# Linear attention with a token and a channel mixer: all operations in another explicit order, batch 1's sums of values ahead of the first channel mix, two thirds of the clamps on GpSimd

## The chip, the core and the metric

The kernel runs on one core of one Trainium2 chip. The metric is the device time of one execution in microseconds (us). The core has TensorE (PE, matrix products, with its weight loads as PEld), VectorE (DVE), ScalarE (ACT), GpSimd (POOL), and the queue engine SyncE (SP), which issues nearly all transfers. Each engine runs its own instructions in the order in which they stand; engines wait for one another by semaphores.

## What is computed

The reference takes `q`, `k`, `v` of 4 batches, 4 heads, 1088 positions and 32 dimensions, two sketches `S1`, `S2` (8 x 32), and four mixer weights that come in as float32. Cut to what matters:

```python
phi(x) = einsum('i,j->ij', S1 x, S2 x)            # 64 features per position
kv  = einsum('bhsf,bhsd->bhfd', phi(k), v);  z = phi(k).sum(s)
x   = (phi(q) @ kv) / (phi(q) @ z + 1e-6)         # (4, 1088, 128)
h   = relu(x.T @ w_tok1) @ w_tok2                 # token mixer: 1088 -> 256 -> 1088
u   = x + h.T
out = u + relu(u @ w_ch1) @ w_ch2                 # channel mixer: 128 -> 1536 -> 128
```

## The kernel before, in words

**Inputs.** The four weights arrive as 64-bit doubles and are turned to float32 by integer steps in `convert` (names `w<weight><piece>`: weight 0 and 1 are the token mixer's, 2 and 3 the channel mixer's). The steps of a piece are `.abs` (L270 on DVE or POOL, L272 on ACT), `.low` (L276, ACT), `.sign` (L281 on ACT, L284 on DVE), `.clamp` (L287, DVE or POOL), `.merge` (L290, DVE) and `.add` (L294 or L296, POOL). A piece is then split in a high and a low half, `.hi` (L377, ACT) and `.lo` (L380, DVE or POOL), so that a float32 product is made as three fast matmuls. There are 20 pieces, so 20 clamps beside that of the sketch `s`.

**Stages of a batch b.** `Kb.p0` and `Kb.p4` (L407, PE) project the keys, `Kb.c0` and `Kb.c4` (ACT L418) copy, `Kb.v0`, `Kb.v4`, `Kb.v8` (DVE L428) make the 64 features. **`Kb.s` (L448, PE) sums keys times values**: for b > 0 that is one run of 72 small matmuls; the profile records each float32 matmul in two passes, so it counts 144. `Kb.kvz` (ACT L457) takes the result. `Qb` makes the query features (batch 0 by `Q0.p`, `Q0.a` and `Q0.m`; later batches by `Qb.p`, L497, and by transfers `Qb.w` and `Qb.r`, L606 to L622). `Ab.x` (L652, PE, 72 recorded matmuls of 66 columns) gives numerators and denominators, `Ab.d` (DVE L663 to L666) divides, `Ab.t` (L702 for batch 0, L708 else) and `Ab.w` (L824, L828) are the token mixer, `Ab.hT` its transpose, `A0.u` (L733) adds the residual, `A0.uh` and `A0.ul` (ACT L799, DVE L802) split u.

**The channel mix** `Ui` works on spans of 384 (the last two: 288) columns of u; three spans are batch 0's. For each of its 12 pieces of the hidden size, `Ui.f` (L878) is three matmuls into a bank `ps_h`, `Ui.h` (ACT L882) takes the relu, `Ui.l` (DVE L885) the low half, and `Ui.s` (L891) three matmuls into `ps_o`. A group of three such matmuls is called a **triple** below; there are 288 triples in the kernel, 12 x 12 x 2. `ps_h` has three banks, and the `.sign` step on ACT takes one as well, so that `Ui.f` and the conversion of the weights pass the banks on to each other.

**The order.** `ORDER` (L63 and on) is a list of all operations by name; `Plan.run` emits them in it, and so it decides the order on each engine, on the transfer queues, and, where a name carries `:dve`, `:pool` or `:act`, the engine. `fill:n` puts n matmuls without use on PE, which keep it from standing idle; eight more stand at the very start. No instruction is computed by another rule: the lines that set it are

```python
        for entry in ORDER:
            name, _, e = entry.partition(":")
...
            op = named[name].pop(0)
...
            op.emit(e or next(iter(op.ways)))
```

Of the kernel before, what the change touches and what calls it, by code (L numbers as in the profile page):

```python
# [63 lines left out]
d00 s d10 q0 s.low s.abs w00.low w00.abs:dve s.sign:dve s.clamp s.merge s.add w00.clamp:pool Q0.s0:pool w00.sign:dve w00.merge w00.add w10.abs:act  # L64
w10.low Q0.s1:act d01 w10.clamp:dve w10.sign:act w10.merge w01.abs:dve w10.add w01.low fill:4 Q0.p00 Q0.p01 Q0.a00 Q0.a01 w01.sign:act Q0.m00 Q0.m01
w01.clamp:dve w01.merge Q0.p20 Q0.a20 k0 d02 K0.p0 K0.p4 Q0.p21 K0.c0 s.rows w02.abs:pool w02.clamp:pool K0.c4 w02.low Q0.a21 d04 w02.sign:act v0
K0.v0 Q0.m20 K0.v8 Q0.m21 K0.v4 d03 q1 d05 fill:2 Q0.p10 Q0.p11 K0.s00 K0.s04 K0.s08 K0.s10 K0.s14 K0.s18 w04.abs:act Q0.a10 Q0.a11 w04.low w01.add
w02.merge w02.add w04.clamp:dve Q0.m11 Q0.m10 w03.abs:act w03.low w04.sign:act K0.kvz w03.clamp:dve w05.abs:dve w05.clamp:pool w04.merge w03.sign:act
Q1.p d13 w03.merge Q1.c0 w05.low Q1.c1 w13.abs:act w05.sign:act w13.low w13.sign:act A0.x0 w04.add d11 d12 d30 d20 k1 d21 d22 d14 d31 d32 q2 d23 v1
Q1.w0 Q1.w1 d15 d33 w03.add A0.d0 A0.x1 w13.clamp:dve w05.merge A0.d1 w13.merge w05.add A0.x2 A0.t0 A0.d2 A0.t1 A0.t2 w11.abs:act w11.low w12.low  # L70
w12.abs:act w30.abs:act w11.sign:act w30.low w12.sign:act w30.sign:act A0.relu w13.add K1.p0 A0.hT K1.p4 w11.clamp:dve w20.abs:dve w12.clamp:dve
w30.clamp:dve w11.merge w12.merge w30.merge w20.clamp:pool w11.add w20.low K1.c0 w20.sign:act w12.add w30.add w21.abs:act w21.low K1.c4 A0.hTh
w21.sign:act w22.low w30.hi K1.v0 w20.merge w20.add w20.hi w20.lo:pool w22.abs:act K1.v4 w21.clamp:dve w30.lo:dve K1.v8 w21.merge fill:1 A0.u0 A0.u1
A0.w0 A0.w1 A0.uh00 w22.sign:act w31.abs:act A0.ul00 w22.clamp:dve w14.abs:dve U0.f U0.f Q2.p w21.add w21.hi w21.lo:pool w22.merge w22.add A0.uh11
A0.ul11 U1.f U0.h w31.low U0.l U0.h U0.l w32.low w32.abs:act w31.clamp:dve w31.sign:dve w14.clamp:dve w32.clamp:dve w31.merge U1.h w22.hi w32.sign:act
# [926 lines left out]
```

## Time and profile before

| | |
|---|---|
| time, median of 3 runs | 217.52 us (216.55 to 217.95) |
| time of the profiled execution | 218.62 us |
| span in its profile | 216.8 us |
| PE busy | 209.7 us, 97% of the span |
| DVE, ACT, POOL busy | 144.9, 118.7, 64.5 us |

A slice of the page is 1/40 of the span. PE counts as busy from the start of a matmul to its modelled end, so that a stretch of matmuls that wait a little for one another still reads as busy; what the stretch is worth is read from the start of one group to the start of the next. A row of the timeline merges neighbouring instructions of one line: its start, its length, the engine, and in brackets the idle time ahead of it with what ended it.

### The profile page before, as it was taken

The page shows a single profiled execution, that of the slowest core. Times are in us where ns is not written, and L with a number is a line of the kernel's source. Part 1 is how long each engine was busy: PE and PEld are TensorE (multiplying, and loading weights), DVE is VectorE, ACT ScalarE, POOL GpSimd, SP SyncE. Part 2 cuts the span into 40 slices and gives each one's busy share as a digit, 9 for nine tenths or more (in the row PEclk, how much of TensorE's full clock was granted, in tenths as well). Part 3 has the DMA queues.
Part 4 walks back from the last instruction along what each step waited for, and adds up shares of the span by engine and source line. Part 5 has one row for each costly group of instructions (what it writes and reads, how often), then busy time and mean ns, then how long its engine had stood idle before and what let it go on. Part 6 is the DMA issues. An engine that isn't in the chain of part 4 may idle for free.

```text
span 216.8 us, 5259 instructions
## 1 busy us (share of the span) xinstructions
PE 209.7 (97%) x2069; PEld 195.0 (90%) x2069; DVE 144.9 (67%) x305; ACT 118.7 (55%) x282; POOL 64.5 (30%) x73
## 2 busy tenths in 40 slices
...
GB/s 229 399 407 399 402 357 204 194 179 248 29 216 242 197 165 17 108 186 238 182 101 0 3 3 60 172 61 0 30 5 2 42 36 3 24 0 0 51 0 54
DMA packets 11472, 28.44 MB, mean 131 GB/s; under 512 B 1336, under 2 KB 5432, under 8 KB 11448
## 3 DMA queue, kind: packets, MB, share of 16 engines
q1 hardware_dynamic: 11304, 27.85, 41.1%
q8 instruction: 16, 0.26, 0.5%
q10 hardware_dynamic: 144, 0.26, 0.4%
...
## 4 chain that ended last, share of the span: by engine, by line
PE 87%; DMA 4%; DVE 2%; issue 2%; SPq 2%; ACT 1%; ACTq 0%
PE ps_h L878 34%; PE ps_o L891 33%; DMA doubles<-wt 4%; PE ps_a L708 4%; PE ps_a L828 4%; PE ps_a L652 3%; PE ps_a L448 2%; PE ps_a L824 2%; SPq L252 1%; PE ps_a L702 1%; PE ps_a L407 1%; DVE c L290 1%; PE ps_a L497 1%; DVE k_p L428 1%; PE ps_a L733 1%
## 5 line engine op out<-in xcount | busy, mean ns | idle before, releaser
L885 DVE SCALAR_TENSOR_TENSOR hl<-ps_h,hh 128x384 fp32r<-128x384 f32 (+2 forms) x144 | 74.9, 532 | 59.6 <-ACT hh L882 58.5
L882 ACT ACTIVATE hh<-ps_h 128x384 fp32r<-128x384 f32 (+2 forms) x144 | 67.7, 475 | 75.4 <-PE ps_h L878 54.5
L878 PE MATMUL ps_h<-uh,halves 128*128 128x384 f32 (+2 forms) x288 | 87.6, 335 | 0.0
L891 PE MATMUL ps_o<-hh,halves 128*128 128x384 f32 (+2 forms) x288 | 71.5, 330 | 0.0
L878 PEld LDWEIGHTS ps_h<-uh,halves 128*128 128x128 f32 x288 | 53.8, 190 | 1.0 <-ACT hh L882 0.4
L891 PEld LDWEIGHTS ps_o<-hh,halves 128*128 128x128 f32 x288 | 50.6, 189 | 0.2
L878 PE MATMUL ps_h<-ul,halves 128*128 128x384 f32 (+2 forms) x144 | 47.7, 331 | 0.0
L891 PE MATMUL ps_o<-hl,halves 128*128 128x384 f32 (+2 forms) x144 | 47.3, 328 | 0.0
L878 PEld LDWEIGHTS ps_h<-ul,halves 128*128 128x128 f32 x144 | 27.4, 190 | 0.2 <-DVE ul L802 0.2
L891 PEld LDWEIGHTS ps_o<-hl,halves 128*128 128x128 f32 x144 | 27.2, 189 | 0.0
L802 POOL TENSOR_TENSOR ul<-us,uh 128x320 fp32r<-128x320 f32 (+3 forms) x8 | 6.6, 821 | 57.6 <-ACT uh L799 47.4
L294 POOL TENSOR_TENSOR whole<-c,tail 128x384 int32<-128x384 int32 (+3 forms) x12 | 11.8, 995 | 9.1 <-DVE c L290 7.8
L676 POOL TENSOR_TENSOR xl<-x,xh 128x384 fp32r<-128x384 f32 x7 | 7.1, 1019 | 22.6 <-ACT xh L672 22.6
L632 POOL TENSOR_TENSOR qp<-qp,br 128x544 f32<-128x544 f32 x8 | 10.9, 1369 | 6.2 <-PE ps_o L891 4.5
L428 DVE TENSOR_TENSOR k_p<-ps_a,a_sb 128x1024 f32<-128x1024 f32 (+1 forms) x12 | 11.4, 950 | 0.5 <-ACT a_sb L418 0.4
L276 ACT ACTIVATE tail<-doubles 128x256 int32<-128x256 uint32 (+3 forms) x20 | 10.9, 552 | 0.7 <-DMA doubles<-wt 0.7
L652 PEld LDWEIGHTS ps_a<-kvz,qp 128*64 128x64 f32 x288 | 8.9, 137 | 2.0 <-issue 0.9
L652 PE MATMUL ps_a<-kvz,qp 128*64 128x66 f32 x288 | 9.8, 223 | 0.5 <-issue 0.3
L290 DVE SCALAR_TENSOR_TENSOR c<-c,ps_h 128x512 int32<-128x512 int32 (+3 forms) x17 | 9.3, 559 | 1.1 <-ACT ps_h L281 0.8
L708 PE MATMUL ps_a<-halves,xh 128*128 128x256 f32 x54 | 9.9, 280 | 0.0
L281 ACT ACTIVATE ps_h<-doubles 128x512 int32<-128x512 f32 (+3 forms) x17 | 9.2, 543 | 0.0
L380 POOL TENSOR_TENSOR halves<-whole,halves 128x384 fp32r<-128x384 f32 (+3 forms) x7 | 8.1, 1177 | 2.4 <-ACT halves L377 2.4
...
## 6 DMA issues: line engine op xcount, KB each, us to landing
...
```

The costliest lines, as they stand in the source:

```text
L276: nc.scalar.activation(t["tail"], low.bitcast(U32), AF.Copy, scale=2.0 ** -29)
L281: nc.scalar.activation(t["sign"], f32(high), AF.Prelu, scale=2.0 ** -19, alpha=2.0 ** 70)
L290: nc.vector.scalar_tensor_tensor(t["c"], t["c"], 3, t["sign"], op0=ALU.logical_shift_left, op1=ALU.bitwise_or)
L294: engines[e].tensor_tensor(dst(), t["c"], t["tail"], op=ALU.add)
L428: nc.vector.tensor_tensor(t["k_p"][:pn, t0 * H:t1 * H], a.unsqueeze(3).broadcast_to([pn, n, R, R]), t["sb", base][:pn, at:at + n].unsqueez ...
L632: engines[e].tensor_tensor(qp[:, p, cs], qp[:, p, cs], t["br"][:, p, cs], op=ALU.mult)
L652: nc.tensor.matmul(x_ps[c:c + 64, o:o + 2 * (D + 1)], lhsT=qp[:, p, s0 + c:s0 + c + 64], rhs=kvz_all[b % 2][:, p, :], start=True, stop=True,)
L708: nc.tensor.matmul(t["h_ps"][:, :DTOK], lhsT=t[l][:m, i, :], rhs=part(0, piece, r, j * DTOK, DTOK)[:m], start=(i == 0 and k == 0), stop=(i ...
L878: nc.tensor.matmul(h_ps[:, :cn], lhsT=part(2, at[2][e][0], l, at[2][e][1] * P, P), rhs=r[:, :cn], start=(m == 0), stop=(m == 2))
L882: nc.scalar.activation(t["hh"][:, :cn], t["h"][:, :cn], AF.Relu)
L885: nc.vector.scalar_tensor_tensor(t["hl"][:, :cn], t["h"][:, :cn], 0.0, f32(t["hh"][:, :cn]), op0=ALU.max, op1=ALU.subtract)
L891: nc.tensor.matmul(outs[i][:, :cn], lhsT=part(3, at[3][e][0], l, at[3][e][1] * P, P), rhs=r[:, :cn], start=(e == 0 and m == 0), stop=(e == ...
```

## The change

The table `ORDER` is replaced as a whole; no other line differs. One pair of places of it:

```diff
@@ -61,53 +61,53 @@
 ORDER = """
...
-U1.l w32.merge w31.add w14.low w31.hi w14.sign:act Q2.c0 U0.s U0.s w14.merge K1.s U0.f U0.f U1.s w22.lo:pool w31.lo:pool w32.add U0.h w15.low U0.h
...
+w20.lo:dve w31.abs:dve w31.clamp:pool fill:2 A0.u0 A0.w0 w22.abs:act w30.hi w31.low w21.merge w21.add w22.clamp:pool A0.uh00 A0.ul00 K1.s A0.u1 U0.f
...
```

All 288 triples, all transfers and all steps of the conversion are still there. There is one `fill` more (eight in place of seven beside the first eight). Of the 20 clamps of the weights, POOL has 14 (5 before) and DVE 6 (15 before). DVE has nine `.abs` (seven before) and one `.sign` (three before), and it makes one of the two spreads of the sketch that POOL made.

On TensorE, here is the place of batch 1's sums (L448) in the program before; `whole` and `halves` are converted weights, `hTl` the token mixer's hidden layer:

```order
L497 MATMUL ps_a<-q_sb,s_rows 32x272 x8
L878 MATMUL ps_h<-uh,halves_511 128x384
L878 MATMUL ps_h<-ul,halves_511 128x384
L878 MATMUL ps_h<-uh,halves_511 128x384
L891 MATMUL ps_o<-hh,halves_505 128x384 x2
L891 MATMUL ps_o<-hl,halves_505 128x384
L891 MATMUL ps_o<-hh,halves_505 128x384 x2
L891 MATMUL ps_o<-hl,halves_505 128x384
L448 MATMUL ps_a<-v_sb,k_p 32x33 x72
L878 MATMUL ps_h<-uh,halves_564 128x384
```

and in the change, where it is followed by the rest of the token mixer:

```order
L733 MATMUL ps_a<-ident,x 128x128 x3
L824 MATMUL ps_a<-whole_287,hTl 128x384
L824 MATMUL ps_a<-whole_491,hTl 128x384
L448 MATMUL ps_a<-v_sb,k_p 32x33 x72
L733 MATMUL ps_a<-ident,x 128x128 x3
L878 MATMUL ps_h<-uh,halves_509 128x384
L878 MATMUL ps_h<-ul,halves_509 128x384
L878 MATMUL ps_h<-uh,halves_509 128x384
L824 MATMUL ps_a<-whole_516,hTl 128x384
L824 MATMUL ps_a<-whole_441,hTl 128x384
```

The sums stand behind five triples of the channel mix before, and ahead of the first one in the change; the token mixer's second chunk (`A0.w1`, the last two rows) went behind the first triple. In matmuls as the profile counts them, 336 stand ahead of the sums before and 299 in the change. `A0.w2` (the third chunk) stands behind 17 triples and `A1.x` behind 36 in both.

On GpSimd, this is the conversion of the token mixer's weights in the program before (L287 are clamps, L294 adds):

```order
L294 TENSOR_TENSOR whole_285<-c,tail 128x256
L294 TENSOR_TENSOR whole_288<-c,tail 128x512
L287 TENSOR_SCALAR c<-c 128x256
L294 TENSOR_TENSOR whole_346<-c,tail 128x512
L294 TENSOR_TENSOR whole_369<-c,tail 128x512
L294 TENSOR_TENSOR whole_398<-c,tail 128x256
L294 TENSOR_TENSOR whole_448<-c,tail 128x384
L287 TENSOR_SCALAR c<-c 128x256
L294 TENSOR_TENSOR whole_482<-c,tail 128x384
```

and in the change:

```order
L287 TENSOR_SCALAR c<-c 128x512
L294 TENSOR_TENSOR whole_314<-c,tail 128x512
L287 TENSOR_SCALAR c<-c 128x512
L294 TENSOR_TENSOR whole_333<-c,tail 128x512
L287 TENSOR_SCALAR c<-c 128x256
L294 TENSOR_TENSOR whole_422<-c,tail 128x512
L287 TENSOR_SCALAR c<-c 128x384
L294 TENSOR_TENSOR whole_426<-c,tail 128x256
L294 TENSOR_TENSOR whole_441<-c,tail 128x384
L287 TENSOR_SCALAR c<-c 128x384
L294 TENSOR_TENSOR whole_491<-c,tail 128x384
```

A clamp now stands ahead of nearly every add. On SyncE's queue, the transfers around batch 1's values (`v_sb`; `q_sb` here is batch 2's) stand like this before:

```order
L252 DMA k_sb<-kT 128x1152
L252 DMA doubles_94<-wc 128x256
L252 DMA doubles_98<-wc 128x512
L252 DMA doubles_102<-wt 128x320
L252 DMA doubles_95<-wc 128x256
L252 DMA doubles_99<-wc 128x512
L252 DMA q_sb<-qT 128x1088
L252 DMA doubles_100<-wc 128x512
L252 DMA v_sb<-v 128x1188
```

and in the change:

```order
L252 DMA k_sb<-kT 128x1152
L252 DMA doubles_94<-wc 128x256
L252 DMA doubles_98<-wc 128x512
L252 DMA doubles_95<-wc 128x256
L252 DMA v_sb<-v 128x1188
L252 DMA doubles_102<-wt 128x320
L252 DMA doubles_99<-wc 128x512
```

The values moved ahead of three pieces of weights and of batch 2's queries.

## Rows read from the trace of the kernel before

**Rows 1.** The page, busy time of each engine (its share of the span, and the number of instructions).

```profile
PE 209.7 (97%) x2069; PEld 195.0 (90%) x2069; DVE 144.9 (67%) x305; ACT 118.7 (55%) x282; POOL 64.5 (30%) x73
```

**Rows 2.** Busy time of each engine in three stretches that follow each other; the last three numbers are TensorE's granted clock, the share of the DMA engines' time, and what they moved in GB/s.

```profile
14.00:29.50 15.50, 14.31 (x208) 10.62 (x205) 14.50 (x34) 14.19 (x37) 10.84 (x13) 1.00 1.03 400
29.50:45.10 15.60, 13.96 (x217) 12.59 (x216) 11.29 (x26) 12.76 (x30) 8.08 (x9) 0.89 0.84 219
45.10:213.60 168.50, 168.47 (x1551) 165.12 (x1550) 109.03 (x225) 81.77 (x193) 39.10 (x36) 1.00 0.29 83
```

**Rows 3.** TensorE's timeline, the rows around the start of the channel mix (L878, L891), around batch 1's sums (L448) and at the third chunk of the token mixer (L824, 45.09).

```profile
21.38 2.96 PE L702 MATMUL ps_a<-whole,x 128*128 128x256 f32 x12 [0.21 <-DVE x L666]
24.27 0.69 PE L407 MATMUL ps_a<-s_c,k_sb 128*64 128x64 f32 x16
...
26.58 0.88 PE L733 MATMUL ps_a<-ident,x 128*128 128x128 f32 x6 [0.20 <-DVE k_p L428]
27.30 2.75 PE L824 MATMUL ps_a<-whole,hTl 128*128 128x384 f32 x8
29.58 0.63 PE L878 MATMUL ps_h<-uh,halves 128*128 128x384 f32 x1
...
31.01 0.69 PE L497 MATMUL ps_a<-q_sb,s_rows 64*32 64x272 f32 x16
...
33.40 1.59 PE L448 MATMUL ps_a<-v_sb,k_p 128*32 128x33 f32 x138
36.63 0.26 PE L448 MATMUL ps_a<-v_sb,k_p 128*32 128x33 f32 x6 [1.64 <-issue]
36.82 0.44 PE L878 MATMUL ps_h<-uh,halves 128*128 128x384 f32 x1
...
41.09 0.51 PE L891 MATMUL ps_o<-hh,halves 128*128 128x384 f32 x2
...
42.15 0.49 PE L733 MATMUL ps_a<-ident,x 128*128 128x128 f32 x3
42.40 0.60 PE L891 MATMUL ps_o<-hh,halves 128*128 128x384 f32 x2
...
45.09 1.24 PE L824 MATMUL ps_a<-whole,hTl 128*128 128x320 f32 x4
```

**Rows 4.** The chain of waits, two pieces of the dense part (start, length, what; x6 is two triples).

```profile
50.57 1.04 PE ps_o L891 x6
51.61 0.52 PE ps_h L878 x3
```

**Rows 5.** Busy time in two short stretches, columns as in rows 2: the one with the sums, and the one behind it.

```profile
33.40:36.80 3.40, 1.76 (x145) 1.60 (x144) 2.33 (x6) 2.68 (x7) 2.57 (x3) 1.00 0.79 216
36.80:41.10 4.30, 4.30 (x22) 4.28 (x17) 1.44 (x4) 2.43 (x5) 2.15 (x3) 0.60 1.01 194
```

**Rows 6.** TensorE's timeline, the attention of batch 0 in two pieces (x59 and x13 of 72 matmuls).

```profile
16.58 2.23 PE L652 MATMUL ps_a<-kvz,qp 128*64 128x66 f32 x59 [0.16 <-ACT kvz L457]
19.11 0.57 PE L652 MATMUL ps_a<-kvz,qp 128*64 128x66 f32 x13 [0.30 <-issue]
```

**Rows 7.** The page's row of the queue that carries instructions (packets, MB, share), and the same queue's row in two windows of half a microsecond, 33.5 to 34.0 and 40.5 to 41.0 us; its windows beside these have no row.

```profile
q8 instruction: 16, 0.26, 0.5%
...
q8 instruction: 1, 0.02, 16.2%
...
q8 instruction: 1, 0.02, 20.2%
```

**Rows 8.** DVE's timeline, from the last division of batch 0 to the split of its first chunk of u.

```profile
22.16 0.56 DVE L666 TENSOR_TENSOR x<-ps_a,rec 128x384 f32<-128x384 f32 x1
...
23.22 0.75 DVE L287 TENSOR_SCALAR c<-c 128x384 f32<-128x384 f32 x2
23.89 1.33 DVE L290 SCALAR_TENSOR_TENSOR c<-c,ps_h 128x384 int32<-128x384 int32 x3
25.30 1.23 DVE L428 TENSOR_TENSOR k_p<-ps_a,a_sb 128x1024 f32<-128x1024 f32 x1
...
28.10 0.42 DVE L380 TENSOR_TENSOR halves<-c,halves 128x256 fp32r<-128x256 f32 x1
28.44 0.42 DVE L428 TENSOR_TENSOR k_p<-ps_a,a_sb 128x256 f32<-128x256 f32 x1
28.77 0.41 DVE L290 SCALAR_TENSOR_TENSOR c<-c,ps_h 128x256 int32<-128x256 int32 x1
29.30 0.56 DVE L802 TENSOR_TENSOR ul<-ps_a,uh 128x384 fp32r<-128x384 f32 x1
```

**Rows 9.** A clamp on DVE and what GpSimd did meanwhile, from the two engines' timelines.

```profile
18.69 1.37 DVE L287 TENSOR_SCALAR c<-c 128x384 f32<-128x384 f32 x1
...
17.33 2.52 POOL L294 TENSOR_TENSOR whole<-c,tail 128x512 int32<-128x512 int32 x2 [0.19 <-DVE c L290]
```

**Rows 10.** Groups by line and shape (times seen, then busy us and mean ns of one): clamps on the two engines.

```profile
L287 DVE TENSOR_SCALAR c<-c 128x512 f32<-128x512 f32 x5 | 2.4, 471 | 0.0
L287 POOL TENSOR_SCALAR c<-c 128x256 f32<-128x256 f32 x3 | 1.2, 415 | 4.2 <-DVE c L270 4.2
L287 POOL TENSOR_SCALAR c<-c 128x512 f32<-128x512 f32 x2 | 1.2, 615 | 1.5 <-DVE c L270 1.4
```

**Rows 11.** The page's group of the channel mix's low halves on DVE (columns as in rows 10; what stands behind the bar is idle time ahead of them and its releaser).

```profile
L885 DVE SCALAR_TENSOR_TENSOR hl<-ps_h,hh 128x384 fp32r<-128x384 f32 (+2 forms) x144 | 74.9, 532 | 59.6 <-ACT hh L882 58.5
```

More of the change, by code (lines that the diff above doesn't have):

```diff
@@ L63 @@
 ORDER = """
[L64 to L75, printed above, removed]
@@ L108 @@
-U10.h U10.l U10.h U10.l U11.f U11.f U10.s U11.h U11.l U11.h U11.l U11.h U11.l U11.f U10.s U11.h U11.l U11.f U11.s U10.f U11.s U10.f U11.s U11.s U11.h
-U11.l U10.h U10.l U10.h U10.l U10.f U10.h U10.l U11.f U11.s U10.s U11.f U11.f U10.s U11.h U11.l U10.s U11.f U11.h U11.h U11.h U11.l U11.l U10.ol U11.l
-U11.s U11.f U11.h U11.s U11.s U11.s U11.l U11.s U11.ol U10.out U11.out
+d00 s q0 d01 k0 d10 v0 d02 s.low s.abs s.sign:dve s.clamp s.merge s.add Q0.s0:dve w00.low Q0.s1:act w00.abs:act w00.sign:act w01.abs:dve
@@ new lines @@
+w01.clamp:pool w00.clamp:pool w00.merge fill:4 Q0.p00 Q0.p01 w01.low Q0.a00 Q0.a01 Q0.p20 w01.sign:act Q0.a20 Q0.m00 Q0.m01 w01.merge w10.abs:pool
+w10.clamp:pool w00.add w01.add K0.p0 K0.p4 K0.c0 w10.low K0.c4 s.rows Q0.a21 w10.sign:act Q0.p21 K0.v0 K0.v4 w10.merge d03 K0.v8 Q0.m20 Q0.m21
+w02.abs:act w02.low w02.sign:act d04 fill:1 K0.s00 fill:1 K0.s04 Q0.p10 K0.s08 K0.s10 Q0.p11 K0.s14 K0.s18 Q0.a10 w03.low w04.low w03.abs:dve
+w02.clamp:dve w02.merge w04.abs:dve w10.add q1 d13 d05 w03.clamp:pool Q1.p w03.sign:act Q0.m10 w03.merge Q0.a11 K0.kvz Q0.m11 w04.sign:act w02.add
@@ new lines @@
+w04.clamp:pool w04.merge Q1.c0 Q1.c1 w05.abs:act w05.low w13.abs:act w13.low w05.sign:act w13.sign:act w03.add d11 d20 d30 d12 A0.x0 A0.x1 A0.d0 A0.d1
+A0.x2 A0.t0 A0.t1 w05.clamp:pool w05.merge k1 d21 d22 d31 v1 d14 d32 Q1.w0 Q1.w1 q2 d15 d23 d33 Q1.r0None Q1.r00 Q1.r01 Q1.r1None Q1.r10 Q1.r11
+w04.add w13.clamp:pool w13.merge w05.add A0.d2 w11.abs:act w11.low w11.sign:act w20.low w13.add A0.t2 K1.p0 K1.p4 w20.abs:dve w12.abs:act w30.low
+w12.low w20.sign:act w12.sign:act A0.relu K1.c0 w11.clamp:dve w30.abs:dve w11.merge w20.clamp:dve w30.clamp:dve w12.clamp:pool w20.merge w12.merge
```

68 lines of the change are left out of this document (37 added, 31 removed).

## The prediction

> **What bounds the kernel now.** I read the page first, then the engines' busy time by stretches, then TensorE's timeline. TensorE is busy for 209.7 of 216.8 us [rows 1], which says little by itself, so the stretches matter. From 45.1 us on it is busy for 168.47 of 168.50 us at full clock [rows 2]: there nothing but TensorE's own work counts, and both kernels have the same work. What a new order can win lies ahead of that. From 14.0 to 29.5 us DVE is busy for 14.50, ACT for 14.19 and GpSimd for 10.84 of 15.5 us while the transfers run at 400 GB/s [rows 2]: the weights are converted there, and TensorE waits for what comes out. From 29.5 to 45.1 us TensorE is busy for 13.96 of 15.60 us at a granted clock of 0.89 [rows 2].
>
> TensorE's timeline shows the largest hole. Batch 1's sums start at 33.40, 138 of their 144 matmuls run, then TensorE stands for 1.64 us, with no engine named, and six more run from 36.63 [rows 3]. Behind it the granted clock falls: 0.60 in the mean of 36.8 to 41.1 us, a mixture of the levels 2.4 and 1.2 GHz, against 1.00 until 36.8 [rows 5].
>
> **A point where the two can be compared.** `A0.w2`, the third chunk of the token mixer, stands behind 17 triples of the channel mix in both orders, and ahead of it the same other work is done (but for one fill). Before, it starts at 45.09 [rows 3]. If it starts earlier in the change and nothing new waits behind it, the whole kernel ends earlier by as much.
>
> **What is lost before that point.** From the first triple (29.58) to 45.09 there are 15.51 us [rows 3]. The work in them: 17 triples at 0.52 us [rows 4] are 8.84; the query projection `Q2.p` 0.62 (31.01 to 31.63, its row is 0.69 long with the overlap); the sums 1.6 (1.59 for 138); `A0.u2` 0.25 (42.15 to 42.40) [rows 3]. That makes 11.3, and 4.2 us are lost. Of these 1.64 are the hole. The slow clock costs 1.67: from 36.82 to 41.09, 4.27 us [rows 3], five triples ran, worth 2.60 [rows 4]. Some 0.9 are small waits, half of it at the first triple, whose low half of u is ready only at 29.86 [rows 8].
>
> **Why the hole is there, and whether it stays.** The engine waits for nothing the profile names, in the middle of one run of matmuls that no wait divides. The instruction queue has 16 packets for the kernel, 0.26 MB [rows 7], with 2069 matmuls and as many weight loads [rows 1]: a packet for about 129 matmuls. One starts between 33.5 and 34.0, the next between 40.5 and 41.0 [rows 7]. The hole comes after 336 + 138 = 474 matmuls (336 stand ahead of the sums). A smaller stop of 0.30 us, also without a releaser, comes after 59 of the 72 matmuls of batch 0's attention [rows 6], which 162 matmuls precede: 221. The distance is 253, two packets within the records' errors. So I read the hole as TensorE running out of instructions at a packet's border. Borders are then near 346 and 474: the sums cover 336 to 480, take 128 matmuls in 1.42 us, and reach the second border before the packet has come, which takes 1.42 + 1.64 = 3.06 us.
>
> In the change 299 matmuls stand ahead of the sums. The border at 346 falls inside them, the one at 474 comes 31 matmuls after their end, behind `A0.u1`, `A0.w1`, `A0.u2` and seven triples. From border to border that is 97/144 of 1.6 = 1.1, and 0.44 + 1.14 + 0.25 + 3.64 = 5.5 (half of 0.88 and half of 27.30 to 29.58 for the first two [rows 3]), 6.6 us in place of 1.42. So the hole and the slow clock behind it should be gone: 3.3 us.
>
> The Trainium skill has a rule on this, in "Runtime: NRT & Kernel Launch", section "Instruction fetch mechanics": instructions come in blocks of 256 while the previous block runs, and crossing a block's border is mostly hidden. By that rule the hole would be no matter of the border and would go wherever the sums go; it would leave the sum 3.3 us worse. The distance of 253 matmuls [rows 6] agrees with blocks of that size, the 1.64 us [rows 3] don't agree with "hidden".
>
> **What the change costs ahead of the first triple.** Batch 1's sums now stand in front of it, so they wait for their own inputs with the whole channel mix behind them. Values: they were queued behind 1.9 MB more (three weight pieces and batch 2's queries); at 400 GB/s [rows 2] they land 4.7 us sooner, so no wait is likely for them. Products: `K1.v0`, `v4`, `v8` on DVE. I take the end of `A0.t2` as unchanged (24.3, 21.38 + 2.96 [rows 3]), since the loads, the query features and the divisions that feed it stay in their sequence; bounds 23.6 and 25.0, as DVE does fewer clamps but GpSimd more.
>
> Between the last division (22.16 + 0.56) and `K1.v0` (25.30) DVE has one abs, three clamps and three merges [rows 8]; in the change one abs more, which I take as 0.3 (above zero, and below the 0.42 that a split of as many columns takes [rows 8]). So `K1.v0` ends at about 26.8 (before 26.54). `A0.u0` waits for that bank as it did (26.58 [rows 3]) and takes 0.44, `A0.w0` 1.14, to 28.4; the `fill:2` lies inside that wait (uncovered it costs 0.6). On DVE one merge, `v4` and `v8` follow, 0.41 + 1.2 + 0.4 [rows 8]: 28.8. The sums run from 28.8 to 30.4, `A0.u1` to 30.8. DVE meanwhile makes a low half (0.42), an abs, a merge (0.41) and u's low half (0.56) [rows 8], ready near 30.4. **The first triple starts near 30.8, not 29.58**, but with the sums already done.
>
> From there to `A0.w2`: 17 triples 8.84, `Q2.p` 0.62, `A0.w1` 1.14, `A0.u2` 0.25, together 10.85, so 41.65 without any wait. ACT and DVE are near full there and each pass of a bank of `ps_h` through a sign and a merge can hold a triple: I allow 0.5 (before: 0.9), bounds 0 and 2. `A0.w2` starts at 42.15, **2.9 us earlier**.
>
> **The clamps.** Nine go from DVE to GpSimd. DVE gets up to 0.47 us back for each; on GpSimd a clamp takes 0.42 (256 columns) or 0.62 (512) [rows 10], some 4.7 us for nine. None is in the sum: DVE's relief is what keeps `K1.v0` where it was although GpSimd is in its way. That way is seen at 18.69: a clamp of 384 columns took 1.37 us while GpSimd ran two adds until 19.85 [rows 9], where clamps of 512 columns take 0.47 in the mean [rows 10].
>
> **Behind 45 us.** Both engines' pieces moved there, but TensorE waited 0.03 us in 168.5 [rows 2], so a new order can only add: I allow 0.3.
>
> **Sum.** 2.9 - 0.3 = 2.6 us less than the profiled execution's 218.62, so 216.0 for one like it; that execution stands 1.1 above the median of 217.52. From the median: **214.9 us**.
>
> **Rivals.**
>
> *Clamps on GpSimd hold up DVE (slower).* Ten operations of DVE that GpSimd can hold up as at 18.69 stand between the third piece of weights and `K1.v8`. GpSimd, busy for 10.84 of 15.5 us [rows 2], gets about 3.6 us more there (seven clamps at 0.52) and would be at 93%. If half of them wait 0.9 as that clamp did (1.37 against 0.47 [rows 9, 10]), DVE is 4.5 us later, less some 1.5 of relief (four clamps at 0.47, less one abs): the sums start 3 us later with TensorE idle in front of them, and the clock falls as it did behind the hole, 1.67 more. That turns -2.6 into +2.1: 219.6. It decides from 1.0 us of lateness on, where the clock goes with it. Against it: the mean of DVE's five clamps of 512 columns is 0.47 [rows 10], so none of these waited so long. The Trainium skill states this lock in "SBUF — State Buffer", section "SBUF: two separate sides": whichever of the two starts holds the pair of ports for the whole instruction. The row at 18.69 agrees. Chance 0.13.
>
> *The stop stays (no change).* Either the hole belongs to the sums themselves and goes where they go, or the packet comes too late for the new place as well: behind the hole the next one starts 4 us after the border (36.63 to 40.5 [rows 3, 7]), and if it needs the 2.6 us from 34.0 to 36.63 again, that is 6.6 us, just the time there is. Then an idle stretch of up to 1.6 and the slow clock come back: 3.3 - 2.6, 218.2; with a shorter stop 217. The rule of the Trainium skill quoted above, "Runtime: NRT & Kernel Launch", stands on the side of the first half of this rival. Chance 0.16.
>
> *A new wait in the dense part (no change).* `A2.t0` stands 7 triples behind `A2.x`, before 19. Its cover is 3.6 us. On DVE two divisions (at least 0.56 each, their last step) and a low half (0.42 for 256 columns, here 384) [rows 8] stand in it, some 1.8 at the least; with four low halves of the mix among them (0.53 each [rows 11]) it is 3.9, TensorE idles for 0.3 or more, and where the clock falls too some 2.2 are gone: 217.1. Chance 0.13.
>
> **Chances and range.** The forecast has 0.58; its own range is 213.4 (no wait ahead of `A0.w2`, front 0.7 earlier, nothing lost behind) to 216.2. A measurement of this kernel can tell about 1% (2.2 us) from no change; of the 0.58 some 0.50 lies beyond that. Faster 0.50, slower 0.16 (the first rival and a little of the others), the same 0.34. For 8 in 10 the range goes from 213.2 to 219.0, which leaves out most of the first rival.
>
> **What would show it.** In the profile of the change: the sums start near 29 and run in one piece of 144; the first triple near 30.8; no granted clock below 1.00 from 30 to 45 us; `A0.w2` near 42.2; from there to the end 168.5 us as before. The forecast is wrong if TensorE stands for over 1 us ahead of the sums, if an idle stretch without a releaser comes some 31 matmuls behind them, or if waits appear beyond 45 us.

## The result and the profile after

The changed kernel takes 218.86 us (median of 12 executions, 218.18 to 219.80), the kernel before 217.59 in the same session (12 executions, 216.55 to 222.46). The ratio is 1.0061 with a 95% interval of 1.0040 to 1.0081: 0.6% slower, where 214.9 us had been forecast. The time lies inside the range of 213.2 to 219.0, at its upper end, and on the wrong side of no change. Beside two of the experiments the ratio was 1.0047 (1.0021 to 1.0074) and 1.0021 (0.9983 to 1.0058).

Ratios leave out executions that stand over 1.5% above the fastest of their kernel, and the kernel before has many of those. Of its 90 executions beside the experiments 38 had a granted clock of 0.997 or more and took 217.1 to 220.1 us (median 217.8); the other 52 had a lower one and took 219.0 to 229.0 (median 222.0). Over all 90 the median is 220.5. All 30 executions of the changed kernel, those of the result included, had 0.997 or more and took 217.8 to 220.0 (median 218.9). So the changed kernel is about 1 us slower than an execution of before at full clock, and steadier.

The profiled execution of the changed kernel took 218.18 us, its span is 216.4. The page's busy row and row of the granted clock (tenths, 40 slices), answering to [rows 1]:

```profile
PE 209.7 (97%) x2070; PEld 192.8 (89%) x2070; DVE 147.5 (68%) x301; ACT 117.8 (54%) x282; POOL 63.5 (29%) x77
...
PEclk9999999999999999999999999999999999999999
```

The three stretches of [rows 2], in the changed kernel:

```profile
14.00:29.50 15.50, 14.40 (x329) 10.62 (x325) 14.15 (x33) 12.92 (x35) 12.32 (x16) 1.00 1.04 401
29.50:45.10 15.60, 14.42 (x94) 11.21 (x83) 12.43 (x24) 14.70 (x36) 11.25 (x14) 1.00 0.74 224
45.10:213.00 167.90, 167.90 (x1547) 164.36 (x1545) 112.65 (x227) 80.75 (x190) 33.91 (x32) 1.00 0.31 83
```

The clock is 1.00 throughout, and in the middle stretch TensorE is busy for only 0.46 us more than before, although there is no stop: other waits have come in its place. TensorE's timeline shows them (answering to [rows 3]):

```profile
26.77 1.46 PE L824 MATMUL ps_a<-whole,hTl 128*128 128x384 f32 x4
28.15 1.45 PE L448 MATMUL ps_a<-v_sb,k_p 128*32 128x33 f32 x144
29.54 0.55 PE L733 MATMUL ps_a<-ident,x 128*128 128x128 f32 x3
30.77 0.44 PE L878 MATMUL ps_h<-uh,halves 128*128 128x384 f32 x1 [0.68 <-ACT uh L799]
31.36 0.45 PE L878 MATMUL ps_h<-ul,halves 128*128 128x384 f32 x1 [0.15 <-DVE ul L802]
31.65 0.33 PE L878 MATMUL ps_h<-uh,halves 128*128 128x384 f32 x1
31.82 1.45 PE L824 MATMUL ps_a<-whole,hTl 128*128 128x384 f32 x4
33.10 0.49 PE L733 MATMUL ps_a<-ident,x 128*128 128x128 f32 x3
...
40.56 0.34 PE L891 MATMUL ps_o<-hl,halves 128*128 128x384 f32 x1
41.17 0.44 PE L878 MATMUL ps_h<-uh,halves 128*128 128x384 f32 x1 [0.27 <-DVE c L290]
...
43.92 1.24 PE L824 MATMUL ps_a<-whole,hTl 128*128 128x320 f32 x4
```

The sums run in one piece of 144. Then TensorE waits for `A0.uh00`. ACT's timeline says why it is late: `w22.abs` (L272) stands ahead of it and waits 1.86 us for one of the four `c` buffers, which `w20.lo` on DVE gives up when it ends at 28.98 (28.57 and 0.41 long).

```profile
26.74 0.42 ACT L377 CAST halves<-c 128x256 fp32r<-128x256 f32 x1
29.02 0.70 ACT L272 ACTIVATE c<-doubles 128x512 f32<-128x512 f32 x1 [1.86 <-DVE halves L380]
29.63 0.39 ACT L377 CAST halves<-c 128x256 fp32r<-128x256 f32 x1
29.92 0.43 ACT L276 ACTIVATE tail<-doubles 128x256 int32<-128x256 uint32 x1
30.26 0.46 ACT L799 CAST uh<-ps_a 128x384 fp32r<-128x384 f32 x1
```

The pause ahead of 41.17 is a bank of `ps_h` that `w15.merge` (L290, the second one here) gives up late: on DVE it stands behind a low half (L380) of 1.37 us, while GpSimd runs from 39.27 to 40.16 and from 40.28 to 41.31.

```profile
39.34 1.37 DVE L380 TENSOR_TENSOR halves<-c,halves 128x512 fp32r<-128x512 f32 x1
40.64 0.47 DVE L290 SCALAR_TENSOR_TENSOR c<-c,ps_h 128x320 int32<-128x320 int32 x1
...
39.27 0.89 POOL L294 TENSOR_TENSOR whole<-c,tail 128x320 int32<-128x320 int32 x1 [0.38 <-DVE c L290]
40.28 1.03 POOL L380 TENSOR_TENSOR halves<-whole,halves 128x256 fp32r<-128x256 f32 x1
```

So `A0.w2` starts at 43.92, 1.17 earlier than in the profile of before and not 2.9. At the last matmul 0.42 of this is left (212.86 against 213.28).

### The profile page after: what moved, and what is told of

It is laid out like the page before. It is cut to its first block, busy times and chain, and to the rows that moved or that the text cites. A ratio compares the mean times of both kernels' runs of the same rounds, so it can differ in the third digit from the quotient of the medians.

```text
span 216.4 us, 5250 instructions
## 1 busy us (share of the span) xinstructions
PE 209.7 (97%) x2070; PEld 192.8 (89%) x2070; DVE 147.5 (68%) x301; ACT 117.8 (54%) x282; POOL 63.5 (29%) x77
## 4 chain that ended last, share of the span: by engine, by line
PE 84%; DVE 5%; ACT 5%; issue 3%; POOL 1%; DVEq 0%
PE ps_h L878 33%; PE ps_o L891 33%; PE ps_a L708 4%; PE ps_a L828 4%; PE ps_a L652 3%; PE ps_o L248 2%; DVE k_p L428 2%; ACT tail L276 2%; DVE c L290 2%; PE ps_a L407 1%; PE ps_a L448 1%; POOL whole L294 1%; ACT ps_h L281 1%; ACT c L272 1%; PE ps_a L537 1%
## 5 line engine op out<-in xcount | busy, mean ns | idle before, releaser
L885 DVE SCALAR_TENSOR_TENSOR hl<-ps_h,hh 128x384 fp32r<-128x384 f32 (+2 forms) x144 | 74.1, 531 | 42.7 <-ACT hh L882 42.1
L878 PE MATMUL ps_h<-uh,halves 128*128 128x384 f32 (+2 forms) x288 | 86.4, 332 | 1.0 <-ACT uh L799 0.7
L891 PE MATMUL ps_o<-hh,halves 128*128 128x384 f32 (+2 forms) x288 | 71.7, 331 | 0.0
L878 PEld LDWEIGHTS ps_h<-uh,halves 128*128 128x128 f32 x288 | 53.0, 188 | 3.0 <-DVE c L290 1.0
L891 PEld LDWEIGHTS ps_o<-hh,halves 128*128 128x128 f32 x288 | 50.3, 188 | 1.3 <-ACT hh L882 0.7
L878 PE MATMUL ps_h<-ul,halves 128*128 128x384 f32 (+2 forms) x144 | 47.3, 328 | 0.2 <-DVE ul L802 0.2
L891 PE MATMUL ps_o<-hl,halves 128*128 128x384 f32 (+2 forms) x144 | 47.2, 328 | 0.0
L878 PEld LDWEIGHTS ps_h<-ul,halves 128*128 128x128 f32 x144 | 27.1, 188 | 0.4 <-DVE ul L802 0.4
L891 PEld LDWEIGHTS ps_o<-hl,halves 128*128 128x128 f32 x144 | 27.0, 188 | 0.0
L802 POOL TENSOR_TENSOR ul<-us,uh 128x64 fp32r<-128x64 f32 (+3 forms) x6 | 3.4, 577 | 64.9 <-ACT uh L799 64.9
L632 POOL TENSOR_TENSOR qp<-qp,br 128x544 f32<-128x544 f32 x9 | 12.8, 1433 | 10.8 <-DMA br<-rows 10.8
L294 POOL TENSOR_TENSOR whole<-c,tail 128x384 int32<-128x384 int32 (+3 forms) x12 | 11.8, 993 | 1.2 <-DVE c L290 1.2
L290 DVE SCALAR_TENSOR_TENSOR c<-c,ps_h 128x256 int32<-128x256 int32 (+3 forms) x19 | 10.0, 535 | 2.3 <-POOL c L287 1.1
L380 POOL TENSOR_TENSOR halves<-whole,halves 128x384 fp32r<-128x384 f32 (+3 forms) x10 | 10.3, 1054 | 0.1
L296 POOL TENSOR_TENSOR c<-c,tail 128x256 int32<-128x256 int32 (+1 forms) x8 | 8.1, 1009 | 6.9 <-DVE c L290 3.0
L287 POOL TENSOR_SCALAR c<-c 128x256 f32<-128x256 f32 (+3 forms) x14 | 7.7, 551 | 7.3 <-DVE c L270 6.4
```

The costliest lines, as they stand in the source:

```text
L290: nc.vector.scalar_tensor_tensor(t["c"], t["c"], 3, t["sign"], op0=ALU.logical_shift_left, op1=ALU.bitwise_or)
L294: engines[e].tensor_tensor(dst(), t["c"], t["tail"], op=ALU.add)
L380: engines[e].tensor_tensor(halves[w, i][:, 1], f32(whole[w, i] if w < 2 else t["c"]), f32(halves[w, i][:, 0]), op=ALU.subtract)
L632: engines[e].tensor_tensor(qp[:, p, cs], qp[:, p, cs], t["br"][:, p, cs], op=ALU.mult)
L878: nc.tensor.matmul(h_ps[:, :cn], lhsT=part(2, at[2][e][0], l, at[2][e][1] * P, P), rhs=r[:, :cn], start=(m == 0), stop=(m == 2))
L885: nc.vector.scalar_tensor_tensor(t["hl"][:, :cn], t["h"][:, :cn], 0.0, f32(t["hh"][:, :cn]), op0=ALU.max, op1=ALU.subtract)
```

## The experiments

Theory: the stop is a packet's border inside the sums, the change removes it, and the gain is missing because (A) the profile of before held a loss that its median doesn't have, and (B) the new order has waits of its own. Rivals: the stop belongs to the sums or their place; the clamps on GpSimd cost what the order gains.

### Whose stop is it? Counting matmuls

Kernel before, 6 fills fewer and 46 tiny matmuls more ahead of the plan (e2):

```diff
-WARM = 8
+WARM = 2
 FIRST = "d00"
-PAD = 0
+PAD = 46
```

> The kernel before with only the number of matmuls ahead of the plan changed: 2 fills and 46 matmuls of 8 columns in place of 8 fills, so that every matmul of the program stands 40 places later among TensorE's instructions, and batch 1's sums stand at 376 to 520 in place of 336 to 480. Theory P (the stop belongs to the instruction packet's border at 474): the border now falls 98 matmuls into the sums and the stretch between the borders lasts 2 us longer, so that the stop is gone or under 0.3 us; A0.w2 1.6 us earlier than in an undisturbed run of before, 216.0 us. Rival S (the stop belongs to the sums or their inputs): a stop of 1.6 us behind 138 of the sums again, 217.6 us as before.

The place came out as theory P says, the gain did not. TensorE's timeline:

```profile
35.74 1.28 PE L448 MATMUL ps_a<-v_sb,k_p 128*32 128x33 f32 x98
39.04 0.61 PE L448 MATMUL ps_a<-v_sb,k_p 128*32 128x33 f32 x46 [2.02 <-issue]
...
79.29 0.34 PE L828 MATMUL ps_a<-halves,hTl 128*128 128x384 f32 x1
83.90 0.66 PE L828 MATMUL ps_a<-halves,hTh 128*128 128x384 f32 x2 [4.28 <-issue]
```

The stop now comes behind 98 matmuls, 40 earlier, at the same count (474). It lasts 2.02 us, and a second one of 4.28 us follows batch 2's sums, behind 983 matmuls as recorded, about four packets further. The median is 227.4 us (222.4 to 229.5), slower than before.

The changed kernel with 37 tiny matmuls more (e6):

```diff
-PAD = 0
+PAD = 37
```

> The changed kernel with 37 matmuls of 8 columns added behind the 8 fills at the start (0.3 us, while TensorE waits for its first operands), so that batch 1's sums stand at 336 to 480 as in the kernel before, and packet borders lie 10 and 138 matmuls into them. Theory P (border, then a wait until the next packet has been fetched): the sums break behind 138 of 144 matmuls, TensorE stands there for 1 to 3 us, the first triple 1 us or more later than in the changed kernel, 220 to 222 us. Rival S (place among the work around them, not the count, makes the stop): the sums in one piece, time as the changed kernel.

```profile
28.25 1.74 PE L448 MATMUL ps_a<-v_sb,k_p 128*32 128x33 f32 x138
33.51 0.34 PE L448 MATMUL ps_a<-v_sb,k_p 128*32 128x33 f32 x6 [3.52 <-issue]
```

As theory P says, and more: the stop is there again, 3.52 us behind 138 matmuls, with a second one of 1.84 us later, behind 982 matmuls; 227.0 us (224.8 to 229.3), clock 0.968 to 0.984. Thirty-seven tiny matmuls cost the changed kernel 8 us. With e2 that settles where the stop falls: it goes by the count of matmuls ahead, and not by the place of the sums among the work around them.

### How long it lasts, and what the median of before holds

The kernel before, unchanged (e1, e9, e12):

> The kernel before, unchanged: a second profile of it, and the granted clock of each of its runs. Theory A (the prediction counted on a loss that the median doesn't have): the stop of 1.6 us in batch 1's sums is there again, behind 138 of 144 matmuls, but the granted clock behind it is 1.00, so that A0.w2 starts near 43.4 and the span is near 215.3 (216.8 less the 1.67 us of the slow clock); most of the other runs have a mean clock of 0.998 or more. Theory B (the clock falls whenever the stop is there): clock near 0.6 from 36.8 to 41.1 again, A0.w2 at 45.1, mean clock 0.992 in all runs.

> The kernel before, unchanged, a third profile. Theory A (what the prediction booked as the change's gain is in part a loss of the one profiled execution): in an execution with a clock of 1.00 the stop is there, 1.5 to 1.7 us, without the slow clock behind it, A0.w2 near 43.5, the span 215 to 216; in one with less the first features run slowly (a wait for q_sb ahead of them, 1.65 in place of 1.11 us) or the stop is over 2 us. Theory B: every execution has the stop and 1.67 us of slow clock behind it, as in rows 3 and 5.

> The kernel before, unchanged, a fourth profile on the same chip, to see whether executions differ in the length of the stop and in the clock. Theory A: two profiles differ by one or two of: the wait for q_sb ahead of the first features, a slow clock behind the stop. Theory B: they agree within 0.3 us.

The three took 222.94, 218.21 and 221.62 us, at 0.985, 1.00 and 0.984. Theory A of e1 missed its numbers: that execution has a stop of 3.13 us, a clock of 0.80 over the 8.4 us behind it and `A0.w2` at 48.95, and only 5 of the 17 executions beside it had 0.998 or more. What holds, by e9, is its core: the loss of the one profile isn't in every execution. And executions differ in the length of the stop too: 3.13, 1.54 and 3.44 us. TensorE's timeline and one stretch behind the stop of e9, columns as in [rows 2]:

```profile
30.26 0.63 PE L878 MATMUL ps_h<-uh,halves 128*128 128x384 f32 x1
...
34.10 1.73 PE L448 MATMUL ps_a<-v_sb,k_p 128*32 128x33 f32 x138
37.37 0.26 PE L448 MATMUL ps_a<-v_sb,k_p 128*32 128x33 f32 x6 [1.54 <-issue]
...
44.25 0.97 PE L824 MATMUL ps_a<-whole,hTl 128*128 128x320 f32 x3
...
37.40:44.20 6.80, 6.80 (x45) 6.67 (x46) 4.91 (x11) 5.76 (x14) 3.11 (x4) 1.00 0.88 222
```

The same of e12:

```profile
33.73 1.91 PE L448 MATMUL ps_a<-v_sb,k_p 128*32 128x33 f32 x138
39.08 0.33 PE L448 MATMUL ps_a<-v_sb,k_p 128*32 128x33 f32 x6 [3.44 <-issue]
...
39.10:48.20 9.10, 9.10 (x45) 9.00 (x46) 5.07 (x11) 6.08 (x14) 1.04 (x2) 0.72 0.72 177
```

The execution at full clock (e9) has the stop too, but a clock of 1.00 behind it (0.60 in [rows 5]), and `A0.w2` at 44.25, where three profiles of the changed kernel have it at 43.92, 44.05 and 44.60. In the following table the border's time is counted from the start of the sums with their pace; the packet's is the window of 0.1 us that has a row of the instruction queue, as in [rows 7]. Those rows for e9 (35.0 to 35.1 us) and e12 (36.4 to 36.5):

```profile
q8 instruction: 1, 0.02, 59.9%
...
q8 instruction: 1, 0.02, 80.9%
```

| execution | border passed (346 where none is named) | packet | TensorE goes on | stop, us |
|---|---|---|---|---|
| before, [rows 3, 7] | 33.5 | 33.7 | 36.63 | 1.64 |
| e9, before | 34.2 | 35.0 | 37.37 | 1.54 |
| e1, before | 35.7 | 37.5 | 40.51 | 3.13 |
| e12, before | 33.8 | 36.4 | 39.08 | 3.44 |
| e2, shifted | 32.4 | 36.2 | 39.04 | 2.02 |
| e2, border 858 | 75.8 | 81.3 | 83.90 | 4.28 |
| e6, changed and shifted | 28.4 | 30.9 | 33.51 | 3.52 |
| changed kernel | 28.6 | 31.6 | - | none |

From the packet to the next matmul it is 2.4 to 3.0 us in all seven stops (and 2.6 in e8 and e10, further down). From the border to the packet it is 0.2 to 5.5 us. The share of the DMA engines in that time was 0.29 and 0.27 in the first two rows, where the packet came within 0.8 us, and 1.02, 0.89, 0.78, 0.91 and 1.04 in e1, e12, e2 (twice) and e6, where it took 1.8 us or more. The stop is these two together, less the time for which the packet in hand lasts. In the changed kernel the packet is as late (3.0 us), but TensorE reaches the border at 474 only at 37.25, over 2.6 us after it could have been ready.

The changed kernel again, on another chip (e5, some ten minutes later and not on another day); this gave the second ratio above:

> The changed kernel, unchanged: its time beside the kernel before on another day's chip, with the granted clock of every run. Theory A (the change's gain is that it is spared the stop and the slow clock that before has in some executions; where before has neither, it is no faster): the changed kernel is at 218 to 219.5 with a clock of 0.998 or more in every run; before scatters with its clock, and its runs with a clock of 1.00 are at 216.5 to 218. Theory B (the order is slower by itself everywhere): 0.5% or more above before's median again, whatever before's clocks are.

218.79 us (217.81 to 219.40), clock 0.997 or more in all six; before beside it: nine executions at 0.998 or more, 217.3 to 218.1, and ten below, 220.8 to 226.7. Both theories had a part: the order is slower than an execution of before at full clock, and steadier than all of them taken together (median of all 19: 220.76).

### The sums in two halves

Of the long lines of `ORDER` only the words around an edit are shown, here and below.

```diff
+            if b == 1:
+                first = plan.add(f"{n}.s0", {"pe": 575.0}, sums(0, 0, NT), products + [v_loaded[b]], [kv_hold], [kp_hold, v_hold[b]], boost, 5)
+                last = plan.add(f"{n}.s1", {"pe": 575.0}, sums(1, 0, NT), products + [v_loaded[b]], (), [kp_hold, v_hold[b], kv_hold], boost, 5, order=[first])
+            else:
...
-K1.s U0.f U0.f U1.s
+K1.s0 U0.f U0.f U1.s
...
-U1.f U1.f U0.s U0.s A0.u2
+U1.f U1.f U0.s U0.s K1.s1 A0.u2
```

> The kernel before with batch 1's sums in two halves of 72 matmuls: the first half where the sums stood, the second 7 triples later, ahead of A0.u2; nothing else moved. Theory P (a packet of 128 matmuls is run through in 1.4 us when it holds sums alone, faster than the next can come): the stretch between the borders at 346 and 474 now holds 62 sums, 7 triples and 45 sums, 4.9 us, so that the stop is gone or under a third of what it is in the kernel before on this chip; A0.w2 1.6 us earlier than there or more, about 215.9 us where before is at 217.5, with a clock of 1.00 in nearly all runs. Rival (the stop comes with the packet's arrival, not with the pace): the same stop at the border, now inside the second half, and no gain.

```profile
35.10 0.83 PE L448 MATMUL ps_a<-v_sb,k_p 128*32 128x33 f32 x72
36.29 0.45 PE L882 MATMUL ps_h<-uh,halves 128*128 128x384 f32 x1 [0.36 <-DVE hl L889]
...
40.56 0.83 PE L448 MATMUL ps_a<-v_sb,k_p 128*32 128x33 f32 x72
41.32 0.44 PE L737 MATMUL ps_a<-ident,x 128*128 128x128 f32 x2
```

The stop is gone, although the first half stands where the sums stood and no engine changed. 217.62 us (217.30 to 222.96), ratio 1.0011 (0.9987 to 1.0036); before beside it had 220.76 over all its executions. The forecast of 215.9 was missed: from the first triple (31.25) to `A0.w2` (44.31) it is 13.06 us, against 13.99 in e9, so 0.9 of the 1.54 us came through; the first triple behind the first half waits 0.36 for a low half. In the time nearly nothing is left of it: its six executions with a clock of 0.997 or more have a median of 217.48, the nine of before beside it 217.57.

`q0` moved ahead of `d10` (e10), and both edits (e11, again as e16):

```diff
-d00 s d10 q0 s.low
+d00 s q0 d10 s.low
```

> The kernel before with one load moved: batch 0's queries (q0) ahead of the weight piece d10, as the changed kernel has them; all else as before. Theory Q (in many executions of before TensorE waits 2.3 us for q_sb, its clock falls, and the first features run at 1.65 in place of 1.11 us): no such wait, the first features at 5.5 to 6.4, and the runs with a clock under 1.00 that are left are those with a stop of over 2 us in batch 1's sums; 217.2 us for an undisturbed run, up to 1.5 less than before's median on this chip. Rival: the runs scatter as those of before.

> The kernel before with both: the sums in two halves 7 triples apart, and q0 ahead of d10. If the stop and the wait for q_sb are what separates executions of before, all runs have a clock of 0.997 or more and lie within 1 us of each other, at 215.5 to 217 us, below both kernels. Rival (the halves' own waits and the later weights eat it): 217.5 or more.

> The kernel before with the sums in two halves and q0 ahead of d10, again, beside the three others on one chip: 216.3 to 218.0 and, if what was found holds (the sums' packet is what separates the kernels), 1 to 1.5 us below the changed kernel, and 0.5 us or more below the undisturbed runs of before.

e10: a miss. The wait for `q_sb` was gone, but TensorE waited 1.81 us for ACT's part of `s_spread`, and the profile has a stop of 3.47 us; 222.59 us (220.46 to 223.28). e11: 217.25 (216.28 to 220.11), ratio 0.9932 (0.9894 to 0.9971); e16: 217.45 (216.45 to 220.14), ratio 0.9963 (0.9923 to 1.0002). That is 1.55 us below the changed kernel beside e16 (219.00) and 0.4 to 0.7 below the executions of before with a clock of 0.997 or more (medians 217.99 and 217.84 in the two sessions). Not every execution was at full clock, as e11's forecast had it: 2 of 12 and 3 of 12 had less than 0.997. Nor is every stop gone. In e11's profile one of 1.21 us comes behind 221 matmuls, where the profile of before has 0.30 [rows 6], and in e16's 0.34 us are left at 474, behind 45 matmuls of the second half:

```profile
43.23 0.44 PE L448 MATMUL ps_a<-v_sb,k_p 128*32 128x33 f32 x27 [0.34 <-issue]
```

### The clamps

The changed order with the clamps on the engines of before (e4), and the order of before with the clamps on the new engines (e8):

```diff
-w01.clamp:pool w00.clamp:pool w00.merge
+w01.clamp:dve w00.clamp:pool w00.merge
...
-w10.clamp:pool w00.add w01.add
+w10.clamp:dve w00.add w01.add
```

(13 clamps in all: w01, w10, w04, w03, w13, w12, w21, w22, w31, w14, w23 to DVE, w02 and w20 to GpSimd; e8 is the same the other way.)

> The changed kernel with every clamp on the engine where the kernel before has it (nine more on DVE, nine fewer on GpSimd), the order as it is. Theory G (the clamps on GpSimd cost more than they give: DVE's operations of 0.45 us last 1.2 to 1.4 beside GpSimd's, and w05.add is late): the long DVE rows near 23.6, 39.3 and 44.2 are gone, A0.w2 about 1 us earlier than 43.92, 217.9 us. Rival R (the relief of DVE is needed in the new order): DVE has 9 times 0.47 = 4.2 us more up to 45 us, the products K1.v0 and the first triple come 1 to 2 us later, 220 us or more.

> The kernel before, its order as it is, with every clamp on the engine that the changed kernel gives it (nine more on GpSimd): that part of the change alone. Theory R (DVE's relief pays only where DVE holds up TensorE, and in the order of before it holds it up little; the end is set by TensorE from 45 us on): within 1 us of before. Theory G (GpSimd's clamps hold up DVE and come late themselves): slower by 1 to 3 us, with DVE operations of 1.2 to 1.4 us beside GpSimd's. Theory F (DVE is the bound up to the first triple): the first triple up to 2 us earlier, 216 us.

e4: 224.28 us (223.48 to 225.35), 5.4 above the changed kernel's 218.86 in the session of the result. e8: 225.95 (223.93 to 228.68), ratio 1.0349 (1.0284 to 1.0415). Each part alone is far worse than both together. In e4 the products of batch 0's keys come late; DVE's and TensorE's timeline, and the stretch behind:

```profile
11.07 0.88 DVE L287 TENSOR_SCALAR c<-c 128x384 f32<-128x384 f32 x1 [1.46 <-POOL c L270]
...
13.13 0.87 PE L448 MATMUL ps_o<-v_sb,k_p 128*64 128x33 f32 x16 [1.82 <-DVE k_p L428]
...
14.00:29.50 15.50, 15.37 (x172) 10.63 (x171) 13.37 (x32) 11.01 (x26) 7.57 (x9) 0.69 1.04 401
```

On DVE `w10.clamp` waits 1.46 us for `w10.abs` on GpSimd (which itself starts only when its piece has landed), with those products behind it, and then the clock is at 0.69 in the mean of 15.5 us. In e8 it is `w02.clamp`, 1.85 us for `w02.abs` on GpSimd, and the queries' projection starts at 36.31 where before has 31.01 [rows 3]; the stop then lasts 4.78 us. So the two runs don't price a clamp, and neither G nor R was the reason: what they show is that a clamp on one engine and its `.abs` on another can hold up everything queued behind it.

### The waits of the new order

The changed kernel as the reference (e13); with `w22.abs` and `w22.clamp` behind `A0.uh00` and `A0.ul00` (e3, and again as e14); with `w15.merge` ahead of `w22.lo` as well (e15). The last three of these stood beside each other.

```diff
-A0.u0 A0.w0 w22.abs:act w30.hi w31.low w21.merge w21.add w22.clamp:pool A0.uh00 A0.ul00 K1.s
+A0.u0 A0.w0 w30.hi w31.low w21.merge w21.add A0.uh00 A0.ul00 w22.abs:act w22.clamp:pool K1.s
...
-w15.clamp:dve w22.lo:dve w15.merge
+w15.clamp:dve w15.merge w22.lo:dve
```

> The changed kernel with w22.abs and w22.clamp moved behind A0.uh00 and A0.ul00 in the order, all else as it is. Theory C (ACT's wait of 1.86 us for a c buffer ahead of w22.abs holds up A0.uh00 and with it the first triple): uh00 near 28.5, ul00 near 29.6, the first triple right behind the sums and A0.u1 at 30.0 to 30.2 in place of 30.77, A0.w2 0.6 us earlier (43.3), 218.3 us. Rival D (that time is taken again by the next wait, w22 being later now, or by a bank of ps_h that a merge on DVE gives up late): the first triple earlier but A0.w2 within 0.2 us of 43.92, 218.9 us.

> The changed kernel once more, as the reference for the next two on the same chip: 218.3 to 219.4, the first triple 0.6 to 0.7 us behind A0.u1 (waiting for uh00), A0.w2 13.1 us behind the first triple, and from A0.w2 to the last matmul 168.9 to 169.5 us (theory: the remaining loss of 0.6 us there is the order's) or 168.2 to 168.6 as in the profiles of before (rival: it was those two executions).

> The changed kernel with w22.abs and w22.clamp behind A0.uh00 and A0.ul00, now beside the changed kernel on one chip. Theory C (ACT's wait for a c buffer costs the first triple 0.7 us, and this is carried to the end): from the start of the sums to the start of A0.w1 2.7 to 2.9 us in place of 3.7, 0.5 to 0.8 us below the changed kernel. Rival D (eaten by the next waits): within 0.2 us of it.

> As the one before, and w15.merge on DVE ahead of w22.lo instead of behind it. Theory M (the pause of 0.4 to 0.6 us near 40.6 comes from a bank of ps_h that w15.merge gives up, and this stood behind a low half that lasted 1.37 us beside GpSimd): that pause is gone, A0.w2 0.4 us earlier than without this edit, 217.6 to 218.0. Rival: the bank is free and the triple waits for the next of its inputs (a low half on DVE), no gain.

| | us, median (range) | sums to first triple | first triple to A0.w2 | A0.w2 to last matmul |
|---|---|---|---|---|
| changed (e13) | 219.00 (218.21 to 219.97) | 2.93 | 13.12 | 169.31 |
| + w22 later (e14) | 218.33 (217.08 to 219.40) | 2.02 | 13.19 | 169.52 |
| + w15.merge first (e15) | 217.72 (216.79 to 218.21) | 1.69 | 12.70 | 168.38 |

Theories C and M held: 0.67 and 0.61 us. (e3, with a front 0.9 us later than in the profile after, took 218.47, 217.72 to 218.95.) The column "first triple to A0.w2" alone would not show M: e3, the same kernel as e14, has 12.58 there for 13.19. The pause itself does: it is in the profiles of the changed kernel, e3 and e14, and not in e15. TensorE's rows at the first triple, of e13 and then of e14:

```profile
28.55 1.78 PE L448 MATMUL ps_a<-v_sb,k_p 128*32 128x33 f32 x144
30.26 0.55 PE L733 MATMUL ps_a<-ident,x 128*128 128x128 f32 x3
31.48 0.44 PE L878 MATMUL ps_h<-uh,halves 128*128 128x384 f32 x1 [0.67 <-ACT uh L799]
```

```profile
28.24 1.78 PE L448 MATMUL ps_a<-v_sb,k_p 128*32 128x33 f32 x144
29.96 0.55 PE L733 MATMUL ps_a<-ident,x 128*128 128x128 f32 x3
30.26 0.42 PE L878 MATMUL ps_h<-uh,halves 128*128 128x384 f32 x1
```

In e15 DVE's merge comes first, the low half lasts 0.78 in its new place, and TensorE has no pause there:

```profile
39.54 0.49 DVE L290 SCALAR_TENSOR_TENSOR c<-c,ps_h 128x320 int32<-128x320 int32 x1
39.94 0.78 DVE L380 TENSOR_TENSOR halves<-c,halves 128x512 fp32r<-128x512 f32 x1
...
40.59 0.34 PE L891 MATMUL ps_o<-hl,halves 128*128 128x384 f32 x1
40.77 0.34 PE L878 MATMUL ps_h<-uh,halves 128*128 128x384 f32 x1
```

e15 is 1.3 us below the changed kernel, its ratio to before is 0.9991 (0.9968 to 1.0014), and all 12 executions have a clock of 0.997 or more: as good as an execution of before at full clock, and 1.4 below the median of all 35 executions of before beside it (219.12). Below both kernels by the ratio stands only the version of e11; its second run, e16, has an interval that reaches 1.0002.

## Why the prediction was wrong

**The stop and its cause: right.** It was read from a distance of 253 matmuls and sixteen packets, and it moves by exactly the matmuls that one adds. In the changed kernel, the border at 346 falls inside the sums and the next comes far enough behind. Of the signs named ahead, the sums in one piece, the first triple near 30.8 and the clock of 1.00 came; `A0.w2` near 42.2 and 168.5 us from there to the end did not. The Trainium skill, "Runtime: NRT & Kernel Launch", section "Instruction fetch mechanics", has instructions in blocks of 256, crossings mostly hidden: the stops at 474 (128 matmuls and as many weight loads behind 346) agree with the block, and the 1.5 to 4.8 us show where "mostly" ends, with a block that is run through in 1.4 us.

**The sum against the median: wrong, and the largest term that could have been known.** "3.3 us" took the stop and 1.67 us of slow clock from one execution, and the result was then set 1.1 below, as that execution stood 1.1 above the median. But the slow clock was why it stood there: e9 has none, and lies among the executions at full clock. Of the 90 executions of before none with a lower clock took less than 218.98, so the medians of 217.52 and 217.59 are those of executions without it. Who goes from a profile to a median must not take out a loss that the median lacks. On the median the stop alone was to be had, 1.5 us at most by e9, and e7 shows that little of this reaches the end. Without the 1.67 the prediction's own sum gives 217.52 less 0.93, 216.6.

**"The first triple starts near 30.8": right number, wrong working.** 30.77, 30.90 and 31.48 in three profiles. The sums started earlier than forecast (28.15 for 28.8), and TensorE then stood for `A0.uh00`. The prediction followed DVE up to there and didn't look at ACT's queue, where `w22.abs` waits for a `c` buffer ahead of `A0.uh00`; e14 shows what that cost, 0.67 us of the time.

**"10.85 ... I allow 0.5 (bounds 0 and 2)": mis-sized.** From 30.77 to 43.92 it is 13.15 us, 2.3 above the work. About 0.4 of this is work priced too low: `A0.w1` takes 1.28 (31.82 to 33.10) for 1.14, `A0.u2` 0.39 (33.10 to 33.49) for 0.25, and the triples some 0.53 for 0.52. Another 0.4 is the pause that `w15.merge` makes (40.56 to 41.17, where e15 has 40.59 to 40.77). The rest, some 1.4, is argued from the timeline only: 0.5 behind the late `uh00` and `ul00` in the first triple (in e14 it is 0.4 less, but a new wait of 0.34 for a low half takes most of that), 0.3 for one more bank ahead of 34.90, and gaps of about 0.1 wherever another operation comes between triples.

**"Behind 45 us ... I allow 0.3": too little, and open.** From `A0.w2` to the last matmul it is 168.94 us in the profile of the changed kernel for 168.19 in the one of before, 0.75 more. Two further profiles of the changed kernel have 169.53 and 169.31, three of before 168.66, 168.64 and 168.01. As `A0.w2` comes at about the same time as in e9, this stretch is where the loss shows. That the order makes it isn't shown: e4, with the same order on TensorE, has 168.17, e15, where one merge on DVE moved, 168.38, and e7 and e11, which are the kernel before from `A0.w2` on, have 168.97 and 169.07.

**From 214.9 to 218.86.** 1.77 us for `A0.w2` (43.92 for 42.15), 0.45 behind it (0.75 for 0.3), 1.1 for the step from the execution to the median, and 0.68 by which the profiled execution of the changed kernel lies below its own median: 4.0, with rounding, for 3.96. The last two together, 1.8, are about the 1.67 of slow clock that the median didn't hold.

**The rivals.** *Clamps on GpSimd hold up DVE*: the row exists (1.37 us), but it didn't delay the sums, and it cost 0.4 at `w15.merge`, not 2 to 4. It was also no clamp that stood beside it on GpSimd, but an add (L294) and a split (L380). *The stop stays*: no. *A new wait in the dense part*: not at `A2.t0`, but its kind, the gain given back to waits of the new order, came nearest. Nearest in time was the stop's 218.2, by luck, as the stop didn't stay. The rival that was missing is that an execution of before at full clock is no slower than the changed kernel to begin with.
